# Row sums of exponentials in place of a clamp, values loaded one and a half times, constant matmuls ahead, and a new order by hand

## The chip, the cores and the metric

The kernel runs on one core of one Trainium2 chip. The metric is the time of one execution on the device in microseconds, the median of several runs. Smaller is better.

A core has engines that each work through a list of their own, in order: TensorE (PE in the profile) for matmuls and transposes, VectorE (DVE) and ScalarE (ACT) for elementwise work, GpSimd (POOL) for elementwise work too, and SyncE (SP), which here only issues DMA transfers and, at the end, reads a flag. An instruction waits for what it needs of other engines, and everything behind it on its own engine waits with it.

## The reference

Gated linear attention (a state per head, faded by a sigmoid gate at each step), and then a mixing block: angles, rotation by cosine and sine, mixing over tokens, and a channel product with a ReLU.

```python
f = 1.0 / (1.0 + np.exp(-f_logit))                  # B,H,S,D = 4,8,768,48
for t in range(S):
    state = f[:, :, t, :, None] * state + np.einsum('bhd,bhe->bhde', k[:, :, t], v[:, :, t])
    y[:, :, t] = np.einsum('bhd,bhde->bhe', q[:, :, t], state)
x = y.transpose(0, 2, 1, 3).reshape(B, S, H * D)    # 4, 768, 384
theta = x @ w_theta
zr, zi = x * np.cos(theta), x * np.sin(theta)
yr = np.einsum('ts,bsd->btd', w_tok_r, zr)
yi = np.einsum('ts,bsd->btd', w_tok_i, zi)
u = x + yr + yi
out = u + np.maximum(u @ w_ch, 0.0)
```

All inputs are float32 in value; the weights arrive as 64-bit floats and are decoded on the chip.

## The kernel before

The tokens of each of the four batches are cut into six chunks of 128, 24 in all, numbered through. The attention of a chunk m is written without a loop over time. The four head pairs lie side by side in tiles of 128 x 512.

- Gates: the logits f are loaded (`lf`), clamped from below (`gc`, `gate_clamp`, L236), turned into ln(1 + exp(-f)) by two activations (`go`, L241 and L242), summed along the chunk by a scan (`gs`, L246), and exponentiated twice (`ge`, L253 and L254) into p, the decay from the chunk's start, and its inverse, which overwrites f. `gp` (L257) keeps the last column of p in `pes`. q is multiplied by p (`gq`, L261), k by the capped inverse (`gk`, L266).
- Attention: transposes of k (`ke`, L308) and their copy (`kt`, through L143); scores (`sc`, L297) and their mask (`ma`, L303); sums of keys times values (`up`, L322); the state in the middle and at the end of the chunk (`sa`, L328 or L330, `st`, L334) and its fading (`sm`, L338); the outputs from the old state (`qs`, L353) and within the chunk (`ou`, L361); a copy (`xc`), transposes (`xt`, L371) and a copy into the tile `ut` of the group (`xs`). v of a chunk is one load of 384 KB (`lv`, L520) with two full copies of it in different head orders.
- Angles and rotation: the angle product (`th`, L402), rounding (`tn`, L407 on ScalarE or L409 on VectorE), remainder (`se`, L413), absolute value (`ab`, L418 on ScalarE or L420 on VectorE), two sines (`tr`), the product with x (`ro`, L435). From the second batch on the results are split into a high and a low float32r part (`zh`, `zl`).
- Mixing: `f0`, `f1`, `f2` (L458) are the token products of a chunk's rotated values for the three blocks of 128 columns, accumulated over the six chunks of a batch for one of two groups of 384 tokens. There are eight groups. The first batch multiplies in float32, the others as three float32r products. `v` (L462) adds, `uh` and `ul` (L469) split again, `c` (L476) is the channel product, `cv` (L490) the ReLU and sum, `so` (L494) one of three stores of a group.
- Weights: `lw`, `d1` (L182), `d2` (L187), `d3` (L192 and L193), `di` (L197), `d4`, `d5` (L217), `e4`, `e5` load and decode the weights piece by piece and split them.

What sets the order is a table written by hand, `ORDER`: a long row of these step names, each standing for the next chunk, group or piece of its kind; a suffix /P, /D or /A moves the step to GpSimd, VectorE or ScalarE. The program issues the steps in this order, and each engine keeps it.

The scaled products are exact only while the gates' range is moderate. `fl` (`find_worst`, L501 to L505) reduces `pes` on VectorE, compares, sums the comparison over partitions by a tiny matmul `pf`, and copies the result into `flag`. `rv` (L565) reads the flag into registers of the engines. If it is above zero a slow exact recurrence follows (the branch, L617), else nothing. Behind the branch the last group is stored by one DMA (L650):

```python
fn["rv"] = load_flag
for step in " ".join(ORDER).split():
    step, _, e = step.partition("/")
    m = done[step] = done.get(step, -1) + 1
    here[0] = engines[e]
    fn[step](m)
...
with tc.If(over[0] > 0, preferred_fallthrough_block=False):
...
nc.sync.dma_start(out[B - 1, :, S - TH:].rearrange("(k p) t -> p k t", p=P), uts[LAST])
```

In the trace an fp32 matmul shows as two records, a transpose and a float32r matmul as one; three or six lines of the table often merge into one row there.

## Time and profile before

| | |
|---|---|
| median of 3 runs | 340.54 us (339.99 to 340.63) |
| the profiled execution | 340.03 us |
| its span, first to last instruction | 338.3 us |
| TensorE busy | 320.4 us (95%) |
| VectorE busy | 251.6 us (74%) |
| ScalarE busy | 188.7 us (56%) |
| GpSimd busy | 108.6 us (32%) |
| DMA | 45.54 MB, mean 135 GB/s |

The shares are means over the whole span. The opening, the long stretch in which the products run, and the end have different limits, so the prediction reads stretches and timelines and not the means. A busy time is the time in which an engine's records cover the clock; matmuls overlap in the records, so the time of a block of them, not of one, tells their pace.

### The profile page before, as it was taken

How to read it: one execution, taken by the hardware profiler on the slowest of the kernel's cores; microseconds unless marked ns; L12 is line 12 of the kernel's file. 1: busy time of each engine (PE TensorE's matmuls, PEld its weight loads, DVE VectorE, ACT ScalarE, POOL GpSimd, SP SyncE). 2: the span in 40 equal slices, each digit the busy share in tenths (PEclk: the TensorE clock that was granted, in tenths of full speed). 3: DMA queues.
4: the chain of work that ended last, by engine and by line, in shares of the span. 5: the costliest groups of instructions: out<-in, count | busy, mean ns of one | idle time of the engine just before them, and what ended most of it. 6: DMA issues, size and time to landing. Idle time of an engine off the chain costs nothing. (4 is left out here: it accounts for less than half of the span.)

```text
span 338.3 us, 9998 instructions
## 1 busy us (share of the span) xinstructions
PE 320.4 (95%) x4320; PEld 283.2 (84%) x4320; DVE 251.6 (74%) x411; ACT 188.7 (56%) x308; POOL 108.6 (32%) x105
## 2 busy tenths in 40 slices
PE   0789999999999999999999999999999999999993
PEld 0676766776776789999999999999999999999992
DVE  5989999999999998898987857855437848534211
ACT  6787997995866755588476685244076114400010
POOL 3585152134418235701445423323212201300010
PEclk9999999999999999999999999999999999999998
DMA  7994994738761262374124320532121120000012
GB/s 256 382 401 168 317 372 151 249 114 323 244 224 30 64 230 82 91 233 141 33 85 149 122 79 2 187 114 84 40 73 48 47 73 27 0 2 0 11 60 78
DMA packets 21618, 45.54 MB, mean 135 GB/s; under 512 B 2368, under 2 KB 5440, under 8 KB 21568
## 3 DMA queue, kind: packets, MB, share of 16 engines
q1 hardware_dynamic: 21568, 44.84, 38.5%
q8 instruction: 36, 0.59, 0.7%
q14 instruction: 14, 0.11, 0.1%
HBM read 40.11 MB, written 4.72 MB: 133 GB/s over the span
## 5 line engine op out<-in xcount | busy, mean ns | idle before, releaser
L458 PE MATMUL pm<-wp,z 128*128 128x384 f32 x648 | 118.4, 337 | 0.0
L458 PEld LDWEIGHTS pm<-wp,z 128*128 128x128 f32 x648 | 112.4, 188 | 0.4
L458 PE MATMUL pm<-value,z 128*128 128x384 f32 x144 | 49.3, 487 | 0.0
L476 PE MATMUL pch<-uhl,wch 128*128 128x384 f32 x216 | 40.0, 337 | 0.0
L458 PEld LDWEIGHTS pm<-value,z 128*128 128x128 f32 x144 | 26.4, 190 | 15.2
L476 PEld LDWEIGHTS pch<-uhl,wch 128*128 128x128 f32 x216 | 37.4, 188 | 0.0
L469 POOL TENSOR_TENSOR uhl<-ut,uhl 128x384 fp32r<-128x384 f32 x13 | 14.2, 1094 | 67.0 <-ACT uhl L143 35.5
L236 POOL TENSOR_SCALAR f<-f 128x512 f32<-128x512 f32 x16 | 26.6, 1666 | 13.3 <-DMA f<-in_f_dram 12.5
L246 DVE TENSOR_TENSOR_SCAN f<-carry,f 128x512 f32<-128x512 f32 x24 | 29.8, 1246 | 1.4 <-ACT f L242 1.4
L257 POOL COPY pes<-p 128x4 f32<-128x4 f32 x24 | 10.5, 439 | 52.9 <-ACT p L253 52.9
L490 DVE SCALAR_TENSOR_TENSOR ut<-pch,ut 128x384 f32<-128x384 f32 x24 | 13.1, 550 | 18.8 <-PE pch L476 17.1
L308 PE MATMUL psk<-ident,k 128*128 128x128 f32 x96 | 16.9, 303 | 10.0 <-DVE k L266 10.0
L261 POOL TENSOR_TENSOR q<-q,p 128x512 f32<-128x512 f32 x12 | 17.3, 1446 | 23.1 <-ACT p L253 14.6
L462 DVE TENSOR_TENSOR ut<-pm,ut 128x384 f32<-128x384 f32 x24 | 13.0, 551 | 14.2 <-PE pm L458 14.2
L253 ACT ACTIVATE p<-f 128x512 f32<-128x512 f32 x24 | 15.1, 630 | 14.4 <-DVE f L246 6.8
L402 PE MATMUL pth<-wth,xh 128*128 128x384 f32 x108 | 23.0, 348 | 0.0
L308 PEld LDWEIGHTS psk<-ident,k 128*128 128x128 f32 x96 | 12.2, 153 | 12.3 <-issue 10.3
L435 DVE TENSOR_TENSOR w<-w,x 128x768 f32<-128x768 f32 x18 | 17.2, 962 | 6.3 <-ACT w L426 6.3
L143 ACT COPY x<-py 128x384 f32<-128x384 f32 x19 | 9.1, 478 | 22.5 <-PE py L361 22.1
L361 PEld LDWEIGHTS py<-v,sc 64*64 64x64 f32 x768 | 15.0, 140 | 7.4 <-issue 4.5
L143 ACT CAST uhl<-ut 128x384 fp32r<-128x384 f32 x7 | 3.6, 513 | 31.1 <-DVE ut L462 17.5
L266 DVE SCALAR_TENSOR_TENSOR k<-f,k 128x512 f32<-128x512 f32 x24 | 18.2, 758 | 1.8 <-ACT f L254 1.1
(83 smaller groups left out, 622.6 us busy)
## 6 DMA issues: line engine op xcount, KB each, us to landing
v<-in_v_dram SPq DMA_DIRECT2D x24, 384.0 KB, 4.3
f<-in_f_dram SPq DMA_DIRECT2D x24, 256.0 KB, 3.8
q<-in_q_dram SPq DMA_DIRECT2D x24, 256.0 KB, 4.1
k<-in_k_dram SPq DMA_DIRECT2D x24, 256.0 KB, 4.3
raw<-in_w_r_dram SPq DMA_DIRECT2D x12, 384.0 KB, 5.9
raw<-in_w_i_dram SPq DMA_DIRECT2D x12, 384.0 KB, 6.3
out_dram<-ut SPq DMA_DIRECT2D x21, 192.0 KB, 1.9
raw<-in_w_theta_dram SPq DMA_DIRECT2D x3, 384.0 KB, 6.4
```

The source lines that it names most:

```text
L236: on(nc.vector).tensor_scalar(ft, ft, F_MIN, None, op0=ALU.max)
L246: nc.vector.tensor_tensor_scan(fl, carry[:, pairs(h)].rearrange("p n t -> p (n t)"), fl, 0.0, ALU.mult, ALU.add)
L253: nc.scalar.activation(ps_[m][:, pairs(h)], ft, AF.Exp, scale=-1.0)
L261: on(nc.vector).tensor_tensor(qt, qt, ps_[m][:, pairs(h)], op=ALU.mult)
L266: nc.vector.scalar_tensor_tensor(kt, loaded["f", m][:, pairs(h)], E_TOP, kt, op0=ALU.min, op1=ALU.mult)
L308: nc.tensor.transpose(psks[m][:, p, :], loaded["k", m][:, p, :], ident)
L361: nc.tensor.matmul(out[HALF[t], j, p, :], scs[m][HALF[a], j, p, :], v2[HALF[a], t, p, :], start=(t == 0 and m % NC == 0 and p == 0), stop= ...
L402: nc.tensor.matmul(pths[m], l, r, start=(n == 0), stop=(n == len(ms) - 1))
L435: nc.vector.tensor_tensor(zs[m] if full else w, w, xs[m].unsqueeze(1).to_broadcast([P, 2, DM]), op=ALU.mult)
L458: nc.tensor.matmul(pms[g, d], l, r, start=(s == 0 and i == 0), stop=(s == NC - 1 and i == len(ms) - 1))
L469: on(nc.vector).tensor_tensor(us[g, d][:, 0], uts[g][:, d, :], us[g, d][:, 1], op=ALU.subtract)
L476: nc.tensor.matmul(pcs[g, d], l, r, start=(es[0] == 0 and n == 0), stop=(es[-1] == KD - 1 and n == len(ms) - 1))
```

## The change

- The clamp (`gc`) goes, 8 on VectorE and 16 on GpSimd. In its place the first exponential writes the sums of its rows (`accum_out`) into a new tile `opened`, and `find_worst` also takes the largest of these and compares it with `G_TOP`: on VectorE two small instructions more.
- p and the inverse change places: the inverse decay lies in p, the decay overwrites f.
- The first chunk's gates and its q and k are done in halves of two head pairs (steps with an h ahead).
- v of a chunk is loaded as three blocks of 192 columns in place of two of 384: 288 KB in place of 384.
- 30 matmuls of constants (`wu`, `keep_warm`, 128 x 128, float32) stand in the table ahead of the first angle product.
- The mask's result has two buffers in place of one; the decode step `d2` could run on VectorE, which the table doesn't use.
- `ORDER` is a new table. Among the steps with an engine: `ab/A` 12 to 13, `d4/D` 3 to 2, `d5/P` 5 to 6, `kt/D` 7 to 9, `sm/P` 11 to 13, `tn/D` 9 to 6, `uh/D` 17 to 13, `xs/D` 7 to 9, `zh/D` 8 to 10, `zl/P` 5 to 9, `di/D` 0 to 1. ScalarE loads its function tables 28 times in place of 22. `fl` stands just ahead of the last `c`, and of the 21 single stores two stand behind `rv`, at the very end.

```diff
-F_MIN = -44.0
+G_TOP = 1e18
-CUT = 0
+CUT = 1
 ORDER = (
-    "lf gc lf gc go go gs lf gc/P lq lk lv gs ge gq gp go ge gk lw lk gs ke kt up gp sc lq gq/P d1 lw lq d2 gk ke",
...
-    "f2 f2 ul so f2 cv cv c cv uh ul/P f2 v uh c c ul/P so c so so so rv cv cv cv",
+    "hlf hgo wu wu wu wu lf go hlf hgo hgs hge wu wu wu wu wu wu wu wu gs hlk hlq hlk hgs hgk hge hgk lf ke wu wu",
...
+    "v uh/D ul cv f1 f2 f2 f2 f1 f1 f1 f1 f1 f2 f2 so v c cv c f2 cv c uh/D ul/P v uh/D ul c gp fl c rv cv cv cv",
+    "so so",
 )
+    opened = const.tile([P, B * NC + 1], F32, tag="opened", name="opened")
-    def gate_clamp(m, h=None):
-        ft = loaded["f", m][:, pairs(h)]
-        on(nc.vector).tensor_scalar(ft, ft, F_MIN, None, op0=ALU.max)
-
     def gate_open(m, h=None):
-        nc.scalar.activation(ft, ft, AF.Exp, scale=-1.0)
+        n = B * NC if h else m
+        nc.scalar.activation(ft, ft, AF.Exp, scale=-1.0, accum_out=opened[:, n:n + 1])
         nc.scalar.activation(ft, ft, AF.Ln, bias=1.0)
-        nc.scalar.activation(ps_[m][:, pairs(h)], ft, AF.Exp, scale=-1.0)
-        nc.scalar.activation(ft, ft, AF.Exp)
+        nc.scalar.activation(ps_[m][:, pairs(h)], ft, AF.Exp)
+        nc.scalar.activation(ft, ft, AF.Exp, scale=-1.0)
-        scs[m] = sb.tile([P, 2, NP, HF], F32, tag="sc", bufs=1, name=f"sc{m}")
+        scs[m] = sb.tile([P, 2, NP, HF], F32, tag="sc", bufs=2, name=f"sc{m}")
+    def keep_warm(n):
+
+        nc.tensor.matmul(bank([P, C], f"warm{n}"), ident, carry[:, 1], start=True, stop=True)
+
-    worst = const.tile([P, 2], F32, tag="worst", name="worst")
+    worst = const.tile([P, 3], F32, tag="worst", name="worst")
     def find_worst(_):
         nc.vector.tensor_reduce(worst[:, 0:1], pes, axis=AX.XY, op=ALU.min)
-        nc.vector.tensor_scalar(worst[:, 1:2], worst[:, 0:1], E_MIN, None, op0=ALU.is_lt)
+        nc.vector.tensor_reduce(worst[:, 1:2], opened, axis=AX.X, op=ALU.max)
+        nc.vector.tensor_scalar(worst[:, 0:1], worst[:, 0:1], E_MIN, None, op0=ALU.is_lt)
+        nc.vector.scalar_tensor_tensor(worst[:, 2:3], worst[:, 1:2], G_TOP, worst[:, 0:1], op0=ALU.is_gt, op1=ALU.add)
         pf = bank([P, 1], "pf")
-        nc.tensor.matmul(pf[:1, :], ones, worst[:, 1:2], start=True, stop=True)
+        nc.tensor.matmul(pf[:1, :], ones, worst[:, 2:3], start=True, stop=True)
         nc.vector.tensor_copy(flag[:1, :], pf[:1, :])
-        vs[m] = sb.tile([P, 2, DM], F32, tag="v", bufs=3, name=f"v{m}")
+        vs[m] = sb.tile([P, 3, NP * D], F32, tag="v", bufs=3, name=f"v{m}")
```

Three places of the order follow, a row for each instruction or run of like ones.

VectorE at the start, before: behind four constants come two clamps and two scans, then q and k of the first chunk; `mid` is the copy of the first sums.

```order
L236 TENSOR_SCALAR f_92<-f_92 128x512
L236 TENSOR_SCALAR f_95<-f_95 128x512
L246 SCALAR_TENSOR_TENSOR f_92<-carry,f_92 128x512
L246 SCALAR_TENSOR_TENSOR f_95<-carry,f_95 128x512
L261 TENSOR_TENSOR q_107<-q_107,p_114 128x512
L266 SCALAR_TENSOR_TENSOR k_109<-f_92,k_109 128x512
L246 SCALAR_TENSOR_TENSOR f_104<-carry,f_104 128x512
L182 TENSOR_SCALAR raw_125<-raw_125 128x768
L266 SCALAR_TENSOR_TENSOR k_128<-f_95,k_128 128x512
L328 COPY mid_191<-sk 128x192
```

VectorE at the start, now, up to the same copy (L329); `ktok` is the copy of the transposed k, `raw` and `value` are pieces of weights.

```order
L248 SCALAR_TENSOR_TENSOR f_93<-carry,f_93 128x256
L248 SCALAR_TENSOR_TENSOR f_106<-carry,f_106 128x512
L248 SCALAR_TENSOR_TENSOR f_93<-carry,f_93 128x256
L268 SCALAR_TENSOR_TENSOR k_134<-p_114,k_134 128x256 x2
L268 SCALAR_TENSOR_TENSOR k_158<-p_177,k_158 128x512
L263 TENSOR_TENSOR q_136<-q_136,f_93 128x256
L145 COPY ktok_195<-psk_146 128x512
L184 TENSOR_SCALAR raw_166<-raw_166 128x768
L248 SCALAR_TENSOR_TENSOR f_144<-carry,f_144 128x512
L197 SCALAR_TENSOR_TENSOR raw_166<-raw_166 128x768
L198 SCALAR_TENSOR_TENSOR value_214<-raw_166 128x768
L329 COPY mid_256<-sk 128x192
```

The clamps are gone and the first scan works on half; between the scaled k of chunk 1 and the copy of the first sums there now stand a copy, a decode, a scan and a join pair.

TensorE at the start, before: transposes of k of chunk 0, its sums and scores, transposes of chunk 1, and so on.

```order
L308 MATMUL psk_131<-ident,k_109 128x128 x4
L322 MATMUL sk<-v_111,ktok_136 64x48 x16
L297 MATMUL sk_156<-q_107,k_109 64x64 x16
L308 MATMUL psk_184<-ident,k_128 128x128 x4
L353 MATMUL py_216<-mid_191,q_107 64x48 x8
L322 MATMUL sk_156<-v_205,ktok_200 64x48 x16
```

TensorE at the start, now, from the last of twelve constant matmuls on; `warm` is their result, which nothing reads; of the nine between the two transposes the first and the last are shown.

```order
L501 MATMUL warm_131<-carry,ident 128x128
L310 MATMUL psk_146<-ident,k_134 128x128 x4
L501 MATMUL warm_151<-carry,ident 128x128
...
L501 MATMUL warm_175<-carry,ident 128x128
L310 MATMUL psk_188<-ident,k_158 128x128 x4
L323 MATMUL sk<-v_171,ktok_195 64x48 x16
L299 MATMUL sk_229<-q_136,k_134 64x64 x16
L501 MATMUL warm_246<-carry,ident 128x128
L354 MATMUL py_263<-mid_256,q_136 64x48 x8
L323 MATMUL sk_229<-v_180,ktok_254 64x48 x16
```

The transposes of chunk 1 moved ahead of the sums of chunk 0, and the constant matmuls stand between.

SyncE near the end, before: the last single stores, then the flag and the branch.

```order
L494 DMA out_dram<-ut_2157 128x384 x3
L494 DMA out_dram<-ut_2856 128x384 x3
L494 DMA out_dram<-ut_3272 128x384 x3
L565 TENSOR_LOAD flag
L565 ISA x2
L617 COMPARE_AND_BRANCH
```

SyncE near the end, now.

```order
L496 DMA out_dram<-ut_2167 128x384 x3
L496 DMA out_dram<-ut_2843 128x384 x3
L496 DMA out_dram<-ut_3310 128x384
L573 TENSOR_LOAD flag
L573 ISA x2
L496 DMA out_dram<-ut_3310 128x384 x2
L625 COMPARE_AND_BRANCH
```

Two stores of the group before the last moved behind the flag, and stand between it and the branch. On TensorE the little matmul of the flag, which stood among the token products of the last group, now stands nine matmuls ahead of the last one:

```order
L478 MATMUL pch_4375<-uhl_4383,wch_88 128x384
L478 MATMUL pch_4379<-uhl_4383,wch_88 128x384
L478 MATMUL pch_4379<-uhl_4383,wch_87 128x384
L478 MATMUL pch_4379<-uhl_4383,wch_88 128x384
L512 MATMUL pf<-worst,ones 1x1
L478 MATMUL pch_4371<-uhl_4387,wch_88 128x384
```

Behind it are only the channel products of the last split part.

## Rows read from the trace of the kernel before

**Rows 1.** Stretches: busy us (x instructions) of PE, PEld, DVE, ACT, POOL; clock; DMA; GB/s.

```profile
9.50:31.20 21.70, 19.21 (x329) 14.46 (x329) 19.92 (x30) 16.78 (x29) 13.64 (x12) 1.00 0.90 343
31.20:60.00 28.80, 28.72 (x567) 19.78 (x570) 27.55 (x46) 24.43 (x39) 9.91 (x11) 1.00 0.74 253
60.00:120.00 60.00, 59.86 (x761) 42.67 (x753) 59.22 (x87) 45.23 (x74) 22.94 (x21) 1.00 0.54 184
120.00:200.00 80.00, 80.00 (x1250) 76.82 (x1249) 67.57 (x112) 53.60 (x88) 32.62 (x28) 1.00 0.38 125
```

**Rows 2.** Timeline of the end, all engines: start us, us, engine, line, operation.

```profile
327.59 0.33 SPq L494 DMA_DIRECT2D out_dram<-ut  x1
...
327.79 4.84 PE L476 MATMUL pch<-uhl,wch 128*128 128x384 f32 x27
...
333.43 0.39 SPq L650 DMA_DIRECT2D out_dram<-ut  x1
```

**Rows 3.** Timeline of PE around 31 us: the first two angle products' blocks.

```profile
27.09 4.19 PE L402 MATMUL pth<-value,ut 128*128 128x384 f32 x6
...
34.54 2.20 PE L402 MATMUL pth<-value,ut 128*128 128x384 f32 x6
```

**Rows 4.** Waits of PE up to 31.2: us in total, times, longest.

```profile
PE psk L308 <- DVE k L266: 10.0, 2, 9.6
```

**Rows 5.** Stretches again (columns as in group 1), up to 71.34.

```profile
0.00:71.34 71.34, 59.26 (x1038) 41.87 (x1042) 63.87 (x102) 58.06 (x95) 29.18 (x36) 1.00 0.77 274
```

**Rows 6.** Costliest groups by form: count | busy us, mean ns | idle before.

```profile
L246 DVE TENSOR_TENSOR_SCAN f<-carry,f 128x512 f32<-128x512 f32 x24 | 29.8, 1246 | 1.4 <-ACT f L242 1.4
L236 POOL TENSOR_SCALAR f<-f 128x512 f32<-128x512 f32 x16 | 26.6, 1666 | 13.3 <-DMA f<-in_f_dram 12.5 <-DVE k L266 0.8
...
L266 DVE SCALAR_TENSOR_TENSOR k<-f,k 128x512 f32<-128x512 f32 x24 | 18.2, 758 | 1.8 <-ACT f L254 1.1 <-DMA k<-in_k_dram 0.6
...
L226 ACT ACT_TABLE_LOAD x11 | 14.1, 1283 | 1.0 <-PEq L689 0.8
...
L192 DVE SCALAR_TENSOR_TENSOR raw<-raw 128x768 int32<-128x768 int32 x14 | 13.7, 980 | 0.0
...
L261 DVE TENSOR_TENSOR q<-q,p 128x512 f32<-128x512 f32 x12 | 8.6, 715 | 0.8 <-ACT p L253 0.8
...
L420 DVE TENSOR_SCALAR w<-w 128x384 int32<-128x384 int32 x12 | 5.6, 465 | 0.2
L409 DVE TENSOR_SCALAR w<-pth 128x384 f32<-128x384 f32 x9 | 4.9, 548 | 0.4 <-PE pth L402 0.4
...
L236 DVE TENSOR_SCALAR f<-f 128x512 f32<-128x512 f32 x8 | 3.5, 442 | 4.9 <-DMA f<-in_f_dram 4.9
L338 DVE TENSOR_TENSOR st<-st,pes 128x192 f32<-128x192 f32 x9 | 3.2, 357 | 0.0
```

**Rows 7.** Timeline of DVE, two operations beside GpSimd.

```profile
5.52 2.71 DVE L246 TENSOR_TENSOR_SCAN f<-carry,f 128x512 f32<-128x512 f32 x2 [0.75 <-ACT f L242]
...
30.25 1.69 DVE L266 SCALAR_TENSOR_TENSOR k<-f,k 128x512 f32<-128x512 f32 x1
```

**Rows 8.** Timeline of POOL up to 72 us: clamps and a scaling of q.

```profile
6.41 1.61 POOL L236 TENSOR_SCALAR f<-f 128x512 f32<-128x512 f32 x1 [4.51 <-DMA f<-in_f_dram]
...
29.65 1.74 POOL L261 TENSOR_TENSOR q<-q,p 128x512 f32<-128x512 f32 x1 [0.67 <-DMA q<-in_q_dram]
...
67.06 1.48 POOL L236 TENSOR_SCALAR f<-f 128x512 f32<-128x512 f32 x1
```

**Rows 9.** SyncE's steps at L565, L617, L650; last, landing of L494's stores.

```profile
L565 SPq TENSOR_LOAD <-flag x1: 492/492/492, 328.0 to 328.0; - x1
...
L617 SPq EVENT_SEMAPHORE  x8: 17/17/17, 328.9 to 329.8; - x8
...
L650 SPq EVENT_SEMAPHORE  x5: 17/28/2772, 330.4 to 330.6; - x5
...
DMA to landing us min/median/max: 1.8/1.9/5.2
```

More of the change, by code (lines that the diff above doesn't have):

```diff
@@ L356, in att_out @@
     def att_out(m):
-        out, v2 = y_of(m), vs[m][:, 1, :].rearrange("s (t p e) -> s t p e", t=2, p=NP)
+        out = y_of(m)
         for n, (p, t) in enumerate(OUT):
@@ L360, in att_out @@
                 j = a ^ t
-                nc.tensor.matmul(out[HALF[t], j, p, :], scs[m][HALF[a], j, p, :], v2[HALF[a], t, p, :],
+                nc.tensor.matmul(out[HALF[t], j, p, :], scs[m][HALF[a], j, p, :],
+                                 vs[m][HALF[a], 2 * j, p * D:(p + 1) * D],
                                  start=(t == 0 and m % NC == 0 and p == 0), stop=(p == NP - 1))
@@ L559, in gla_moe_kernel @@
         "f0": piece(0), "f1": piece(1), "f2": piece(2), "v": group(add_u), "uh": group(split_uh), "ul": group(split_ul), "c": channels, "cv": group(finish),
-        "so": group(lambda g, d: store(g // NTH, g, d)), "fl": find_worst,
+        "so": group(lambda g, d: store(g // NTH, g, d)), "fl": find_worst, "wu": keep_warm,
     }
@@ L664, in layout @@
     halves = v.transpose(0, 2, 1, 3).reshape(B, NC, 2, HF, NP, 2, D)
-    rolled = np.stack([np.stack([halves[:, :, t, :, :, a ^ t] for t in range(2)], axis=3) for a in range(2)], axis=2)
-    v2 = np.stack([halves.reshape(B, NC, C, DM), rolled.reshape(B, NC, C, DM)], axis=3)
-    v2 = np.ascontiguousarray(v2)
+    parts = [halves[..., 0, :], halves[..., 1, :], halves[:, :, ::-1, :, :, 1, :]]
+    v2 = np.ascontiguousarray(np.stack([a.reshape(B, NC, C, NP * D) for a in parts], axis=3))
     return {
```

16 lines of the change are left out of this document (9 added, 7 removed), and 66 rows, old and new, of the table ORDER.

## Prediction

> **What bounds the kernel now.** I read the table of stretches first. From 31.2 us on, TensorE is busy 28.72 of 28.80, 59.86 of 60 and 80.00 of 80 us [rows 1], and so to its last matmul, in the block that starts at 327.79 and runs 4.84 us [rows 2]. Time can therefore be won in three ways only: TensorE starts its full stretch earlier, it has less to do, or the end behind its last matmul gets shorter. The change takes no matmul away and adds 30, so the two ends decide.
>
> The second view is TensorE's timeline around 31 us. The angle product of one chunk (L402, three fp32 matmuls 128x384, each of which makes two records) takes 4.19 us at 27.09 and 2.20 us at 34.54 [rows 3]. The granted clock column reads 1.00 in both stretches [rows 1], so it doesn't show the step; the durations do. I read them as the lower of TensorE's two levels (1.2 GHz) up to 31.2 us and the upper (2.4 GHz) after it. TensorE's waits before that are small: two for scaled k, 10.0 us in sum, of which 9.6 stand before its first matmul [rows 4].
>
> The third view is VectorE in the same stretches: 19.92 of 21.70, 27.55 of 28.80, 59.22 of 60, and only after 120 us 67.57 of 80 [rows 1]. So for a third of the run VectorE is as full as TensorE. An earlier TensorE meets the same VectorE, and what it wins stays only as far as VectorE has less to do for the same matmuls. This is the step on which the forecast rests.
>
> **VectorE's list up to one point.** At 71.34 us of before TensorE starts the scores of chunk 7, and VectorE, with 102 instructions (four of them constants) begun, was busy 63.87 us of it [rows 5]. In the new order TensorE has as much work behind it (45.7 us of matmul time at the upper level, by counting both orders, the 30 constant ones left out) when it comes to the outputs of chunk 6, for which VectorE must have done 94 instructions. By kinds, at the mean of one [rows 6]: four clamps at 0.442 less (1.77); one scan at 1.246 less (ten, now eight and two halves); one scaling of k at 0.758 less; three roundings L409 at 0.548 less (1.64), and a copy of the same shape; one fade L338 at 0.357 less; one weight split, at the 0.980 of a join. Together 7.3 us less. More are 1.5 scalings of q at 0.715 (1.07), two joins of a decoded weight at 0.980 (1.96), one L420 and one scaling of a weight, both at 0.465 (0.93). Together 4.0 more. That leaves 3.3 us; but the last instruction that before had begun by then (a q, 0.7) was not needed yet, so I count 2.6. The same count at other points up to 120 us gives 2 to 6, so this is near the least, and the least binds.
>
> **The clamps on GpSimd** go too, 16 at 1.666, 26.6 us [rows 6]. GpSimd itself is not awaited on the path, so they give nothing directly. But VectorE is slower beside it: two scans at 5.52 take 2.71, where two means make 2.49, beside the clamp at 6.41; a scaling of k at 30.25 takes 1.69 instead of 0.758 beside a scaling of q at 29.65, a kind that stays [rows 7, 8]. Up to 71 us eight clamps run there, the last at 67.06 [rows 8]. The relief lies between 0 (the next GpSimd operation slides into the gap) and some 1.5 (0.2 for each as the scans show). I take 0.6, a little under the middle, since GpSimd has other work to put there.
>
> The Trainium skill ("SBUF — State Buffer", Who interferes with whom) states a harder rule: VectorE and GpSimd share one pair of ports, and for an instruction that needs it the other engine is fully blocked while it is held. By it eight clamps would have held VectorE for up to 13 us, and this sum would be rival B at its fullest; the scans beside the clamp lost 0.2 and not 1.6, so the trace doesn't agree as far as that operation goes.
>
> **Other parts of the opening.** The first chunk's gates in halves take out a clamp (0.44), half a scan (0.62) and half a k (0.38) before the first matmul [rows 6], so it comes about 1.5 us earlier, at some 8 us. I don't add this: VectorE's first work still waits for the first f, and the list above already holds it. The 30 constant matmuls are fp32, 128x128: a record three times as wide takes 4.19/6 = 0.70 at the lower level [rows 3], so by my estimate one of them is 2 x 0.23 = 0.47 there and 0.24 at the upper, all of them 14 or 7 us. All stand ahead of the first angle product, where TensorE would mostly wait: twelve before the first transposes of k, from some 1.7 us (the constants are there) to 7.3 at the lower level, nine between the first and the second. If the twelve bring the clock up, the nine take 2.1 and end by the time the second k is scaled, and are free; if not, 4.2, which delays the first sums (rival D). With the clock up, VectorE's own waits for TensorE shrink as well: of its 1.8 us of idle time between 9.5 and 31.2 [rows 1] I take a quarter, 0.4, between nothing and all. v's loads shrink by a quarter; DMA, 0.90 busy there [rows 1], gets room, worth nothing where no load is awaited. ACT gets six more table loads at 1.283 [rows 6], 7.7 us at most on 58.06 of 71.34 [rows 5]: 65.8, still under 68, so hidden. The row sums that the exponential now writes have no row; their price is between 0 and the 0.465 of a small VectorE instruction each, on ACT, hidden likewise; I take 0. Opening: 2.6 + 0.6 + 0.4 = **3.6 us won**.
>
> **The end.** In before the flag has long been computed when SyncE gets to it: it sends the last store of the group before the last (327.59), loads the flag at 328.0, stands in its branch at 328.9, has the stores' landings by 330, waits on L650's semaphores from 330.4 [rows 9], and sends the last store at 333.43, 5.64 after the last 27 matmuls began [rows 2]. All of it lies under TensorE and VectorE. In the new order the worst-case check stands 18 matmuls into these 27, with nine behind it: 18/27 of 4.84 is 3.2 after their begin. The flag's copy and hand-over add 0.25. Then SyncE loads it and gets through in 0.9 (328.0 to 328.9 [rows 9]): 4.4. Only now come two stores, 0.33 to 0.4 each to issue, the second at 4.8; it lands 1.9 later [rows 9], at 6.7. The branch's way out waits for all DMA queues, so it is this landing. From the landing of before (327.59 + 1.9 = 329.5) to the L650 semaphores it took 0.9 to 1.1; so the last store goes out at 7.7, against 5.64. VectorE's last finishing step, which set the 5.64 in before, no longer counts. Cost: **2.1 us**, between 1.7 (landing 0.2 sooner, hand-overs free) and 2.6 (the flag's load on VectorE also delays the finishing steps). Two instructions more in the check cost nothing: they fall under the 18 matmuls.
>
> **Sum.** 340.03, the profiled run, less 3.6, plus 2.1: 338.5. The profiled run lies 0.5 under the median 340.54; carried over to that, **339.0 us**.
>
> **Rivals.**
> A, the forecast: opening 2 to 5, so 337.6 to 340.6.
> B, VectorE doesn't bind: its 1.8 us of idle time close altogether, and the relief is all of 1.5. 2.6 + 1.8 + 1.5 = 5.9 won, 2.1 lost: 336.7. For it speaks that constant matmuls bring the clock up early; against it that VectorE's list is nearly all in series there. The rule of the ports in the skill, named above, would lead here.
> C, slower: VectorE holds TensorE at the old pace, because of one place. Before the copy of the first sums (mid, L328, now L329), the new order puts a decode, a scan and a join pair: 0.65 + 1.25 + 1.96 = 3.9 us [rows 6] (the decode at about two thirds of a join), and the first reads of the state wait behind it. What the list saves is spent by that, the late flag costs its 2.1 and nothing covers it: 342.1 at 0.5 won, 342.6 at none. It decides from the point where the opening gives less than 2.1.
> D, the constant matmuls don't do what they are there for: TensorE stays at its lower level through the first angle product, which then takes 4.2 again [rows 3], and the nine constants take 4.2, so that the 1.5 us of the earlier start are gone before the first sums. Of the opening a third is left, 1.2; 2.1 is lost: 341.4. For it speaks that 15 us of transposes and narrow products before 27.09 (19.21 busy of 21.70, the angle product's 4.1 off [rows 1]) did not raise the clock; against it that the twelve would run without a gap, as the wide products do when the clock rises at 31.2. The skill ("TensorE: Matmul & The Clock Gate", What's actually happening) says that the throttled state is the default and activity releases it; by this the row of before should have been fast earlier than it is, and the trace agrees only in part.
>
> **Chances.** A 0.50, B 0.16, C 0.21, D 0.13. About 0.2% is what a measurement of this kernel can tell from no change: 0.7 us, so faster is below 339.9, slower above 341.2. From A 0.37 fall faster, 0.11 same, 0.02 slower; B is all faster; C 0.17 slower and 0.04 same; D 0.05 same, 0.08 slower. Faster 0.53, same 0.20, slower 0.27. The range runs from 336.4 (B, with the end at 1.8) to 342.3 (C); left out are more than B and the full C with an end of 2.6, 0.15 or so. The likeliest case's own range is 337.6 to 340.6.
>
> **What would show it.** In the trace of after: the first angle product shorter than 2.3 us and starting by about 24 (else D); VectorE's busy share up to 70 us still above 0.9, with TensorE waiting for mask, mid or scaled k (else B); VectorE's scans and k beside GpSimd nearer their means; TensorE's last matmul about 3.6 us earlier; from that to the last store's issue 2.9 instead of 0.8 us, with SyncE in its branch waiting for a store that it issued after the flag. It is wrong if TensorE's waits after 31 us exceed 1 us in sum, or if the last store goes out right after VectorE's last step.

## The result, and the profile after

The changed kernel takes 342.32 us (median of 20 runs, 341.05 to 344.91), the kernel before 340.10 in 20 runs beside it: 1.0072 times as long, 95% interval 1.005 to 1.0095. It is slower by 2.2 us, where 339.0 and a gain were forecast. Two things are to be explained: the end, where two stores now stand behind the flag, and the opening, whose forecast gain of 3.6 us is not in the time. The profiled execution took 343.98 with a span of 341.6, so it is one of the longer ones.

Busy times of the whole span come first (share, instructions). They say little, as in the kernel before: TensorE 95% again, VectorE 4 us less, ScalarE 11 us more, GpSimd 15 less.

```profile
PE 324.7 (95%) x4380; PEld 288.7 (85%) x4380; DVE 247.5 (72%) x398; ACT 199.3 (58%) x345; POOL 94.0 (28%) x97
```

The end is where the clearest loss lies. In the timeline of all engines from 326 us on (start, duration, engine, line; line numbers are those of the changed kernel) the check's little matmul stands between the 18th and the 19th of the last 27 channel products, the two single stores go out at 331.55, and the last store only at 335.77:

```profile
327.06 3.28 PE L478 MATMUL pch<-uhl,wch 128*128 128x384 f32 x18
...
330.27 0.19 PE L512 MATMUL pf<-worst,ones 128*1 128x1 f32 x2
...
330.39 1.83 PE L478 MATMUL pch<-uhl,wch 128*128 128x384 f32 x9
330.50 0.15 DVE L513 CAST flag<-pf 1x1 int32<-1x1 f32 x1 [0.94 <-PE pf L512]
331.31 1.50 DVE L492 SCALAR_TENSOR_TENSOR ut<-pch,ut 128x384 f32<-128x384 f32 x3 [0.67 <-PE pch L478]
331.55 0.81 SPq L496 DMA_DIRECT2D out_dram<-ut  x2
335.77 0.39 SPq L658 DMA_DIRECT2D out_dram<-ut  x1
```

TensorE ends at 330.39 + 1.83 = 332.22, so 0.41 earlier than before (332.63 by [rows 2]); but the last store goes out 3.55 us behind that, against 0.80 there. The row of SyncE's waits says that it stood in the branch (L625, L617 before) in between. The row doesn't name a transfer, but the second of the two stores, out at 332.0, landed at 334.8, and the branch's last semaphore went at 334.9. That this landing is what it waited for is tested by e3 below.

```profile
SPq L625 <- SPq L625: 2.0, 2, 1.2
```

From the last store's issue to the end of the span it takes 5.8 us, against 4.9 before. Together the end is 3.7 us longer.

The opening has to be read in short stretches (columns as in [rows 1]: busy time of PE, PEld, DVE, ACT, POOL; granted clock; DMA share; GB/s):

```profile
8.00:12.00 4.00, 3.20 (x25) 2.72 (x24) 1.75 (x4) 2.60 (x6) 0.88 (x2) 1.00 1.01 354
12.00:15.00 3.00, 1.60 (x67) 1.32 (x66) 2.34 (x3) 1.54 (x2) 0.00 (x0) 1.00 1.07 403
15.00:17.00 2.00, 0.00 (x0) 0.03 (x1) 1.83 (x5) 1.89 (x5) 1.56 (x1) 0.80 0.98 344
17.00:19.00 2.00, 1.99 (x49) 1.91 (x49) 1.16 (x3) 1.32 (x4) 2.00 (x3) 0.50 0.83 289
19.00:21.00 2.00, 2.00 (x12) 1.67 (x16) 2.00 (x5) 0.01 (x1) 0.41 (x2) 0.50 0.88 257
21.00:23.00 2.00, 2.00 (x65) 1.91 (x66) 1.97 (x5) 1.10 (x3) 0.00 (x0) 0.50 0.34 124
23.00:26.00 3.00, 3.00 (x79) 2.70 (x79) 1.40 (x4) 2.97 (x6) 0.19 (x1) 0.99 0.04 15
26.00:32.00 6.00, 6.00 (x145) 4.61 (x145) 5.97 (x9) 5.50 (x13) 1.16 (x2) 1.00 1.01 345
```

The clock column now has something to show. Up to 15 us it is 1.00 and the matmuls have the upper pace (32 narrow ones in 0.68 us below, 1.10 in the kernel before). From 15 to 17 TensorE does nothing. Then the clock is 0.50, the lower of the two levels, until 23 us, while TensorE is busy all the time. The timeline of TensorE shows the pause and whom it waited for, that of VectorE why:

```profile
13.37 0.68 PE L323 MATMUL sk<-v,ktok 64*64 64x48 f32 x32 [1.35 <-DMA v<-in_v_dram]
13.87 0.66 PE L299 MATMUL sk<-q,k 48*64 48x64 f32 x32
...
17.01 0.77 PE L354 MATMUL py<-mid,q 48*64 48x48 f32 x10 [2.06 <-DVE st L335]
...
27.61 2.10 PE L404 MATMUL pth<-value,ut 128*128 128x384 f32 x6
```

```profile
12.66 0.57 DVE L184 TENSOR_SCALAR raw<-raw 128x768 int32<-128x768 int32 x1 [2.07 <-DMA raw<-in_w_theta_dram]
13.14 1.22 DVE L248 TENSOR_TENSOR_SCAN f<-carry,f 128x512 f32<-128x512 f32 x1
14.27 0.93 DVE L197 SCALAR_TENSOR_TENSOR raw<-raw 128x768 int32<-128x768 int32 x1
15.24 0.96 DVE L198 SCALAR_TENSOR_TENSOR value<-raw 128x768 int32<-128x768 int32 x1
16.12 0.35 DVE L329 COPY mid<-sk 128x192 f32<-128x192 f32 x1
```

VectorE's copy of the first sums (L329) could have gone at 14.05, when the products of L323 were there. It went at 16.12, because a decode (L184) ahead of it waited 2.07 us for the load of a weight, and a scan and two joins stand between. These are the four instructions that rival C named. TensorE's first sums had themselves waited 1.35 us, for the load of v. The first angle product runs at the upper level (2.10 us, 4.19 in [rows 3]), but at 27.61, where 24 was expected; it ends 1.6 us earlier than before.

How far TensorE is ahead at any time can be counted. Each matmul record of a trace gets the time that it takes in a closed row at the upper level (0.3225 us for an fp32 record 384 wide, 0.1735 for a float32r one, 0.109 for a transpose, some 0.015 for a narrow one, nothing for a constant one). This gives 299.3 us of work in every kernel here. The work done at a time, less that of the kernel before at the same time, is the lead, in us:

| at | after | e2 | e6 | e3 | e4 | e7 | e11 | e12 |
|---|---|---|---|---|---|---|---|---|
| 26 | -0.9 | 0.8 | 1.1 | -0.4 | -0.3 | 1.8 | 1.8 | -1.2 |
| 44 | 1.7 | 3.7 | 3.4 | 2.4 | 0.8 | 4.3 | 3.7 | -0.4 |
| 62 | 1.7 | 2.7 | 2.0 | 2.1 | 0.4 | 3.5 | 3.5 | -0.1 |
| 112 | 0.9 | 2.4 | 1.6 | 0.9 | -0.2 | 3.5 | 3.5 | -0.8 |
| 136 | 0.7 | 2.1 | 0.2 | 0.7 | -0.4 | 1.2 | 2.4 | -0.8 |
| 328 | 0.7 | 1.2 | 0.0 | 0.5 | -1.2 | 1.0 | 2.4 | -1.0 |

Each column is one execution. The changed kernel, e2 and e3 have the same order up to the last products, and still e2 is up to 2.0 us ahead of the other two. Its TensorE makes the same pause (2.0 us), but its granted clock is 0.86 from 19 to 21 us and 1.00 from 21 on, where the changed kernel has 0.50 until 23. So how long the lower level lasts differs between executions of one order, and a difference of less than 2 us between columns says something only where a wait in the traces stands behind it.

### The profile page after: what moved, and what is told of

It is laid out like the page before. It is cut to its first block, busy times and chain, and to the rows that moved or that the text cites. A ratio compares the mean times of both kernels' runs of the same rounds, so it can differ in the third digit from the quotient of the medians.

```text
span 341.6 us, 10162 instructions
## 1 busy us (share of the span) xinstructions
PE 324.7 (95%) x4380; PEld 288.7 (85%) x4380; DVE 247.5 (72%) x398; ACT 199.3 (58%) x345; POOL 94.0 (28%) x97
## 4 chain that ended last, share of the span: by engine, by line
PE 85%; DVE 5%; DMA 4%; SPq 2%; issue 1%; DVEq 0%
PE pm L460 45%; PE pch L478 11%; PE pth L404 10%; PE py L362 4%; PE py L354 3%; PE sk L299 3%; PE psk L310 3%; PE sk L323 3%; PE pxt L373 2%; DMA raw<-in_w_theta_dram 2%; DMA raw<-in_w_i_dram 2%; SPq L523 1%; SPq L171 1%; PE warm L501 1%; DVE value L198 1%
## 5 line engine op out<-in xcount | busy, mean ns | idle before, releaser
L471 POOL TENSOR_TENSOR uhl<-ut,uhl 128x384 fp32r<-128x384 f32 x13 | 16.3, 1257 | 75.2 <-DVE uhl L145 61.0
L248 DVE TENSOR_TENSOR_SCAN f<-carry,f 128x512 f32<-128x512 f32 (+1 forms) x25 | 31.1, 1253 | 3.7 <-ACT f L244 3.7
L263 POOL TENSOR_TENSOR q<-q,f 128x512 f32<-128x512 f32 (+1 forms) x13 | 19.7, 1518 | 41.2 <-DMA q<-in_q_dram 17.4
L437 DVE TENSOR_TENSOR w<-w,x 128x768 f32<-128x768 f32 x18 | 20.4, 1140 | 4.7 <-ACT w L428 4.5
L259 POOL COPY pes<-f 128x4 f32<-128x4 f32 x24 | 7.8, 326 | 53.9 <-ACT f L256 43.8
L444 POOL TENSOR_TENSOR z<-w,z 128x768 fp32r<-128x768 f32 x9 | 17.3, 1926 | 18.3 <-ACT z L145 14.0
L255 ACT ACTIVATE p<-f 128x512 f32<-128x512 f32 (+1 forms) x25 | 15.3, 612 | 9.2 <-DVE f L248 9.0
L268 DVE SCALAR_TENSOR_TENSOR k<-p,k 128x512 f32<-128x512 f32 (+1 forms) x25 | 17.5, 700 | 3.0 <-ACT p L255 2.0
L404 PEld LDWEIGHTS pth<-wth,xh 128*128 128x128 f32 x108 | 18.7, 188 | 0.9
L354 PE MATMUL py<-mid,q 48*64 48x48 f32 x384 | 16.6, 227 | 2.1 <-DVE st L335 2.1
```

The source lines that it names most:

```text
L248: nc.vector.tensor_tensor_scan(fl, carry[:, pairs(h)].rearrange("p n t -> p (n t)"), fl, 0.0, ALU.mult, ALU.add)
L263: on(nc.vector).tensor_tensor(qt, qt, loaded["f", m][:, pairs(h)], op=ALU.mult)
L268: nc.vector.scalar_tensor_tensor(kt, ps_[m][:, pairs(h)], E_TOP, kt, op0=ALU.min, op1=ALU.mult)
L354: nc.tensor.matmul(out[HALF[t], j, p, :], qt[r, p, HALF[t]], old[t][r, p, :], start=(p == 0), stop=False)
L404: nc.tensor.matmul(pths[m], l, r, start=(n == 0), stop=(n == len(ms) - 1))
L437: nc.vector.tensor_tensor(zs[m] if full else w, w, xs[m].unsqueeze(1).to_broadcast([P, 2, DM]), op=ALU.mult)
```

## The end: e3, e2

Only the two stores moved, the check stays late:

```diff
-    "... uh/D ul/P v uh/D ul c gp fl c rv cv cv cv",
-    "so so",
+    "... uh/D ul/P v uh/D ul so so c gp fl c rv cv cv cv",
```

> The changed kernel with the two last single stores moved ahead of the reading of the flag, the check staying late (nine matmuls ahead of the end). Theory 2a (the two stores behind the flag are the price: the branch waits for their landing): nearly all of what the earlier end gives, 2.3 us or more less than the changed kernel, last store about 1 us behind the last matmul. Rival (the late flag is the price by itself): at most 0.8 less, last store over 2 us behind the last matmul.

339.35 us (337.75 to 340.44, 12 runs), 2.97 under the changed kernel and 0.998 of the kernel before (0.9958 to 1.0002). Its timeline of the end (its lines are one less than in the changed kernel):

```profile
325.29 1.90 SPq L495 DMA_DIRECT2D out_dram<-ut  x2
...
330.35 0.19 PE L511 MATMUL pf<-worst,ones 128*1 128x1 f32 x2
...
330.47 1.83 PE L477 MATMUL pch<-uhl,wch 128*128 128x384 f32 x9
...
331.39 1.50 DVE L491 SCALAR_TENSOR_TENSOR ut<-pch,ut 128x384 f32<-128x384 f32 x3 [0.67 <-PE pch L477]
333.04 0.39 SPq L657 DMA_DIRECT2D out_dram<-ut  x1
```

The flag is as late as in the changed kernel, and the last store goes out 0.74 us behind the last matmul. It is the two stores behind the flag that cost, not the flag. With the check moved early too:

```diff
-    "c f2 ro zh/D f1 zl f1 f2 f2 f0 f0 v v f2 cv v so ...
+    "c f2 ro zh/D f1 zl f1 f2 f2 f0 f0 v v f2 gp fl cv v so ...
-    "... uh/D ul/P v uh/D ul c gp fl c rv cv cv cv",
-    "so so",
+    "... uh/D ul/P v uh/D ul so so c c rv cv cv cv",
```

> The changed kernel with the end of the kernel before: the check of the range (and the copy of the last chunk's decay that it needs) stands among the last token products, and all 21 single stores stand ahead of the reading of the flag. Theory 2 (the end of the changed kernel costs 3.7 us: from TensorE's last matmul to the last instruction 9.4 in place of 5.7): 3 to 3.7 us less than the changed kernel, last store 0.8 us behind the last matmul. Rival (the final transfer is slower for another reason, its landing took 4.9 in place of 3.7): 2.1 to 2.7 less, and the landing stays near 4.9.

339.47 (337.36 to 341.40, 12 runs), 0.9997 of the kernel before (0.9974 to 1.0021): the same as e3. So the two stores behind the flag are the loss at the end, and the flag itself is not (theory 2a). By these medians the end costs the changed kernel 2.9 to 3.0 us; set against the kernel before that ran beside each (340.10 beside the changed kernel, 339.64 beside these two) it is 2.4 to 2.5. The transfer at the very end, 5.8 us from issue to the end of the span, is 5.1 in both, so most of its lengthening goes with the stores as well; why is not shown.

## TensorE's level: e4, b1, e6

All 30 constant matmuls taken out of e3 (every `wu` in the table):

> The changed kernel with its two last single stores ahead of the flag (as in e3_so_only, 339.35) and without any of the 30 constant matmuls. Theory 1 (the constant matmuls lift TensorE's level at about 8 us and win some 3 us ahead of the first angle product, part of which is kept): the first angle product runs at the lower level (about 4.1 us), the time is 1 to 3 us above e3_so_only. Rival (VectorE and the loads set the pace of the opening, TensorE's level is worth nothing): within 0.7 of e3_so_only.

342.19 (10 runs), 2.8 above e3, or 2.4 with each set against the kernel before beside it (340.04 here, 339.64 there). The first angle product of its trace:

```profile
27.82 2.81 PE L403 MATMUL pth<-value,ut 128*128 128x384 f32 x6
```

It takes 2.81 us where the changed kernel has 2.10 and the kernel before 4.19: by this the level rises in the middle of it. The constant matmuls are worth 2.4 to 2.8 us here: in the lead, 1.6 us at 44 and 1.7 at the end. The mirror of it, twelve of them put at the start of the kernel before:

```diff
-    "lf gc lf gc go go gs ...
+    "lf gc wu wu wu wu wu wu wu wu wu wu wu wu lf gc go go gs ...
```

> The kernel before with twelve constant matmuls ahead of its first transposes and nothing else. Theory 1: TensorE's level is up by about 8 us, the first angle product at 27 takes 2.1 in place of 4.2 us or comes earlier, and 1 to 2 us are won against the kernel before. Rival 1 (the level falls again in the first pause, since the rest of the opening has pauses once it runs fast): the granted clock falls back to 0.50 before 20 us, gain under 0.7. Rival 2 (VectorE sets the pace): level stays up, gain under 0.7.

340.26 against 340.04 (ratio 0.9989 to 1.0032): nothing. The stretches of its trace show why:

```profile
8.00:12.00 4.00, 1.78 (x30) 1.41 (x32) 3.64 (x6) 3.79 (x7) 0.86 (x3) 0.64 1.03 403
12.00:15.00 3.00, 3.00 (x66) 2.55 (x64) 2.46 (x6) 1.60 (x4) 1.72 (x2) 0.50 1.05 400
...
26.00:32.00 6.00, 5.76 (x48) 3.26 (x49) 6.00 (x8) 4.28 (x9) 3.13 (x3) 0.50 0.44 164
```

TensorE paused 3.0 us for the first scaled k, the clock fell within 8 to 12 us and stayed at 0.50 past 26. So early matmuls alone don't keep the level up: here, too, it fell behind a pause. That the pause and not their number (12 here, 30 there) decides is argued, not shown.

Eight more constant matmuls in the changed kernel, in TensorE's pause:

```diff
-    "d3 ge kt sa st lv sm qs gp gk ...
+    "d3 ge kt sa st lv sm wu wu wu wu wu wu wu wu qs gp gk ...
```

> The changed kernel with eight constant matmuls more, where TensorE waits for the first state (in front of the first outputs from the state). The wait of VectorE stays as it is. Theory 1: TensorE is busy through 15 to 17 us, the granted clock stays 1.00, the products from 17.0 to 23.8 take half of their time, and the first angle product comes 1 to 3 us earlier; time 1 to 3 us less than the changed kernel. Rival 1 (VectorE alone sets the pace): clock 1.00, but no gain over 0.7 us at the end. Rival 2 (the level falls for another reason than the pause): the granted clock still drops to 0.50 at about 17.

The first half came true:

```profile
15.00:17.00 2.00, 1.40 (x12) 1.41 (x12) 1.86 (x5) 1.92 (x5) 2.00 (x3) 1.00 1.05 418
17.00:19.00 2.00, 2.00 (x57) 1.83 (x57) 1.23 (x3) 0.71 (x2) 1.80 (x2) 1.00 0.92 307
19.00:21.00 2.00, 1.67 (x69) 1.40 (x67) 2.00 (x5) 1.14 (x3) 0.00 (x0) 1.00 0.69 255
```

The clock stays at 1.00, and the first angle product comes at 25.49, 2.1 us earlier than in the trace of the changed kernel. (In e2's trace, whose lower level was short, it comes at 25.68 without the eight matmuls.) But the time is 344.20, 1.9 us more than the changed kernel. No theory had that. VectorE's waits from 24 to 130 us say where the first 1.4 go (waited for, times, longest):

```profile
DVE q L263 <- DMA q<-in_q_dram: 1.9, 2, 1.4
```

The scaling of q of chunk 5 waits for its load at 46 us, where DMA is 1.00 busy from 40 to 44. Set against the changed kernel instruction by instruction, VectorE is 2.1 us ahead at 25 to 36, 1.5 at 37 and 0.6 from 46 on. At 119 us it falls behind, after a wait of 1.84 us on ScalarE for a load of f. In this execution being early only meant waiting there. It explains that nothing is won; the trace ends 0.6 us behind that of the changed kernel, and why the medians differ by 1.9 stays open.

In the 20 runs of the changed kernel the time goes with the level all the same: the mean granted clock over the span tells how long it was low. The six runs at 0.982 to 0.984 take 344.1 in the mean, the eight at 0.988 to 0.990 take 341.5. What else differs between these runs isn't known.

## The first state moved ahead: e1, e10, e12

If the pause is VectorE's wait for the weight, the copy of the sums could go first:

```diff
-    "... hgq ke lk kt/D up d1 lq lq gq/P gs lf lw lw sc wu d2",
-    "d3 ge kt sa st lv sm qs ...
+    "... hgq ke lk kt/D up lq lq gq/P lf lw lw sc wu sa st d1 gs d2",
+    "d3 ge kt lv sm qs ...
```

> The changed kernel with one edit: on VectorE the copy of the first sums and the first state (sa, st) stand ahead of the weight decode, scan and joins (d1, gs, d3), as in the kernel before. Theory 1 (the opening was lost to one wait: TensorE stood from 15.0 to 17.0 us because VectorE's copy of the first sums stood behind a decode that waited 2.1 us for a weight load, and then ran at its lower level to 23.8): the copy comes at about 14.1 in place of 16.1, the granted clock stays 1.00 from 8 to 31 us, and the time falls by 1.5 to 4 us against the changed kernel, to 338.5 to 341 where that has 342.3. Rival (VectorE's list sets the pace in any case, so TensorE's clock there is worth nothing): the first angle product comes earlier, but at the end less than 0.7 us is left.

345.77 (5 runs): 3.4 slower than the changed kernel, both theories wrong. The longest wait of TensorE is now another:

```profile
PE sk L323 <- ACT ktok L145: 3.7, 1, 3.7
```

The scan (`gs`) had moved behind the state, ScalarE's exponentials wait for the scan, and the copy of k's transposes stands behind them. So I put the scan back, and the exponentials and the copy ahead on ScalarE, with the stores of e3:

```diff
-    "... hgq ke lk kt/D up d1 lq lq gq/P gs lf lw lw sc wu d2",
-    "d3 ge kt sa st lv sm qs ...
+    "... hgq ke lk kt/D up lq lq gq/P gs lf lw lw sc wu ge kt sa st d1 d2",
+    "d3 lv sm qs ...
```

> As e3_so_only (339.35), with the copy of the first sums and the first state ahead of the decode and the joins on VectorE, and on ScalarE the exponentials and the copy of k's transposes ahead of the decode's scaling, so that neither stands behind a wait for the weight load (in e1_mid_first the scan and, by it, the copy of k's transposes had been put behind the state, and TensorE waited 3.7 us for that). Theory 1: VectorE's copy of the first sums at about 14.2 in place of 16, no pause of TensorE over 1 us between 12 and 24, the granted clock 1.00 there, and at 62 us 1 us or more further ahead than e3_so_only; time 0.5 to 1.5 us less. Rival (the next products wait for the scaled k or for v instead): a pause of over 1 us elsewhere before 24 and no gain.

341.69, 2.3 slower than e3. The same kernel ran once more, for a trace:

> The same as e10_mid_scan (341.7), for its trace, since the profile of that run was of a disturbed execution. Theory 1 fell there by the time. Theory 5 (what counts is the order in which VectorE gets at the next scaled k and scan, not the first state: with the decode and joins later, the weights are later and the first angle product waits for them): no pause of TensorE between 14 and 17 us, but the first angle product at or after 27.6 with a wait for a weight or for its inputs. Rival (the clock): the granted clock falls to 0.50 before 24 us although the pause at 15 to 17 is gone.

341.99. The copy of the first sums comes at 13.72, 2.4 us earlier than in the changed kernel. What comes then, on VectorE and on GpSimd:

```profile
13.72 0.36 DVE L328 COPY mid<-sk 128x192 f32<-128x192 f32 x1 [1.48 <-PE sk L322]
14.12 0.36 DVE L334 TENSOR_TENSOR st<-sk,mid 128x192 f32<-128x192 f32 x1
...
15.19 1.98 DVE L196 SCALAR_TENSOR_TENSOR raw<-raw 128x768 int32<-128x768 int32 x1 [0.24 <-ACT raw L189]
17.20 2.05 DVE L197 SCALAR_TENSOR_TENSOR value<-raw 128x768 int32<-128x768 int32 x1
...
19.44 0.68 DVE L267 SCALAR_TENSOR_TENSOR k<-p,k 128x512 f32<-128x512 f32 x1
```

```profile
15.08 1.27 POOL L262 TENSOR_TENSOR q<-q,f 128x512 f32<-128x512 f32 x1 [5.84 <-DMA q<-in_q_dram]
16.29 0.92 POOL L258 COPY pes<-f 128x4 f32<-128x4 f32 x1
17.17 1.26 POOL L262 TENSOR_TENSOR q<-q,f 128x512 f32<-128x512 f32 x1
18.38 0.91 POOL L258 COPY pes<-f 128x4 f32<-128x4 f32 x1
```

The two joins take 1.98 and 2.05 us in place of 0.93 and 0.96, each beside a scaling of q on GpSimd. So the scaled k that TensorE needs next goes at 19.44, where the changed kernel had it at 17.47. TensorE waits 3.8 us for it (16.4 to 20.2), and the clock falls to 0.50 from 19 to 24. The first angle product comes at 28.79. The pause only moved, so the level wasn't spared here. In the changed kernel the order is the other way round: the first join is through when q begins on GpSimd at 15.44, the second, issued at 15.24, keeps 0.96, and the q beside it takes 1.89 in place of 1.27. The first theory's cause (the level falls behind a pause) fits these runs as well; its remedy was wrong.

## Where the lead goes: e7, e8, e11

e7 is e3 with the eight matmuls of e6 and the load of q of chunk 5 ahead of two pairs of weight loads:

```diff
-    "... lf sm/P sc sa st lw sm/P qs se ab/A d3 tr ro up sa xt go ma go th lw",
-    "f1 tn d3 f0 gs lq xs lw gq ge ...
+    "... lf sm/P sc sa st lq lw sm/P qs se ab/A d3 tr ro up sa xt go ma go th lw",
+    "f1 tn d3 f0 gs xs lw gq ge ...
```

> As e3_so_only, with the eight constant matmuls of e6_more_wu, and with the load of q of chunk 5 moved ahead of two pairs of weight loads on SyncE's queue. In e6_more_wu TensorE's level stayed up and the first angle product came 2.1 us earlier, but VectorE gave 0.6 back at about 35 us and 0.9 at 46, waiting for loads of q. Theory 3 (what the opening wins is given back to loads that come too late, DMA being 1.00 busy from 40 to 44 us): the wait of 1.4 us at 46 is gone, and VectorE is still 1.5 us ahead of e3_so_only at 60 us; time 1 to 2 us under e3_so_only, 337.4 to 338.4. Rival (another load takes its place, DMA as a whole is the limit): a weight load comes late in its turn, and the time is within 0.7 of e3_so_only.

339.93, 0.6 above e3 (0.2 with each set against the kernel before beside it) and 1.001 of the kernel before (0.9985 to 1.0036). By the time, the rival is the one that held; the trace says more. The wait at 46 us is gone, and the lead is 4.3 us at 44 and 3.5 up to 112, the 3.6 that the forecast gave the opening. By 136 it is 1.2. The timeline between, all engines:

```profile
112.97 2.74 POOL L443 TENSOR_TENSOR z<-w,z 128x768 fp32r<-128x768 f32 x1
...
115.66 0.92 POOL L258 COPY pes<-f 128x4 f32<-128x4 f32 x1
...
116.60 0.33 SPq L522 DMA_DIRECT2D f<-in_f_dram  x1
117.02 0.86 SPq L495 DMA_DIRECT2D out_dram<-ut  x2
...
118.04 0.78 PE L403 MATMUL pth<-wth,xl 128*128 128x384 f32 x3 [0.92 <-POOL xl L394]
...
119.87 0.63 ACT L242 ACTIVATE f<-f 128x512 f32<-128x512 f32 x1 [3.08 <-DMA f<-in_f_dram]
...
120.96 0.56 DVE L144 COPY ut<-pxt 128x384 f32<-128x384 f32 x1 [0.89 <-DMA out_dram<-ut]
```

On GpSimd the small copy of a decay (L258) stands behind a split of 2.74 us. A load of f waits for that copy, to get a free buffer, and goes out at 116.60. Behind it on SyncE stand two stores whose data was ready by 114.6. So ScalarE waits 3.08 us for f and VectorE 0.89 for the stores; TensorE waits 0.92 for another split, which stands behind the same copy on GpSimd. Two ways to mend it. First the copy ahead of the split and the stores ahead of the load:

```diff
-    "... v e5 e5 sm zl/P gp v qs xt go gs go c xs",
+    "... v e5 e5 sm gp zl/P v qs xt go gs go c xs",
-    "... uh/D tn/D se lf so so xt go f2 ge",
+    "... uh/D tn/D se so so lf xt go f2 ge",
```

> As e7_q_early, with two steps of the table moved: two single stores of the first group ahead of a load of f that waits on SyncE for GpSimd's copy of a decay (pes), and that copy ahead of a long split on GpSimd. In e7_q_early TensorE had done 3.5 us more work than in the kernel before at 112 us, and 1.5 at 124: VectorE waited 0.9 us for the stores' landing, ScalarE 3.1 us for the load, TensorE 0.9 for a split behind both. Theory 3 (the opening's gain of 3.6 to 4 us was there, and is given back at single waits for transfers): the lead at 124 is 3 us or more, and the time falls by 1 to 2 us against e7_q_early (339.9), to 338 to 339. Rival (TensorE's lead runs into VectorE's list anyway, as the prediction had it): another wait takes its place by 130 us, less than 0.7 us.

339.83, the same. ScalarE still waited 2.60 us: the load now stood behind the stores, which wait for the ReLU. Then the copy alone (the first of the two edits):

> As e7_q_early with one step moved: the copy of a decay (pes) ahead of a long split on GpSimd, so that the load of f that waits for it on SyncE can go out before the two single stores of the first group and not behind or beside them (in e8_stores_first the stores went ahead and ScalarE still waited 2.6 us for that load). Theory 3 (the opening's lead is given back at single late transfers, here the f at 120 us): ScalarE's wait for f at about 118 is under 1 us, the lead over the kernel before at 136 us is 2.5 us or more (1.2 in e7_q_early), and the time 1 to 2 us under e7_q_early (339.9), so 338 to 339. Rival (VectorE and GpSimd, both full there, take what the load gives): lead at 136 under 1.7, time within 0.7.

338.81 (12 runs; 337.73 to 342.50). ScalarE's row that answers to the one at 119.87:

```profile
117.58 0.63 ACT L242 ACTIVATE f<-f 128x512 f32<-128x512 f32 x1 [0.65 <-DMA f<-in_f_dram]
```

The wait is 0.65, and the lead of 2.4 us at 136 is still there at 328. For that place the lead bears theory 3 out: from 112 to 136 us e7 falls from 3.5 to 1.2 and this run from 3.5 to 2.4. Two other traces point the same way. In e6 the split takes 2.74 us as well, the load goes out at 117.87, and the lead falls from 1.6 to 0.2; in e2 the split takes 1.85, the load goes out at 115.15, and 2.1 of 2.4 are kept. In the time this gain is not shown: the median is 1.1 under that of e7, but the kernel before beside it is lower too (339.59, and 340.04 beside e7), and the intervals of the two ratios overlap. Against the kernel before this best version has a median 0.8 lower, but three of its runs are above 340.5, and the ratio is 0.9998 (0.9964 to 1.0031); that it is faster is not shown.

## Parts alone: b2, b3, e9

The kernel before without its 24 clamp steps:

> The kernel before without its clamp steps (24 gate clamps, 8 on VectorE and 16 on GpSimd, left out; nothing checks the range in their place). This is the part of the change that the prediction priced at 1.77 us of VectorE's list up to 71 us and 0.6 us of relief from GpSimd. Theory (VectorE's list sets the pace of the first 120 us): 1 to 2.4 us less than the kernel before. Rival (loads set it, or TensorE's lower level): within 0.7 of it.

339.90 against 340.04 (0.9967 to 1.0017): nothing like the 2.4 us that the forecast gave. Its profiled execution (342.88) is the slowest of the twelve, so it shows only one way in which a shorter list can be lost: TensorE waits 2.5 us for a scaled k, until 33.0. VectorE is busy throughout from 27 to 33, and one addition to the state, issued at 29.79 beside a scaling of q on GpSimd (1.28 us), takes 1.45 us in place of 0.36. The granted clock is 0.50 from 34 to 38. By the medians, fewer instructions on VectorE did not make this kernel shorter.

The kernel before with v in three blocks (the change's `load_v`, its two readers and the layout):

> The kernel before with one part of the change alone: v of a chunk loaded as three blocks of 192 columns (288 in place of 384 KB), its order untouched. Prediction: v's smaller loads are worth nothing where no load is awaited: within 0.7 of the kernel before, and outside of the span 1.7 us as in the kernel before. Rival 1 (the DMA engines limit the opening of the kernel before as well): 1 us or more less. Rival 2 (the 0.6 us outside of the span come with v's new shape): 2.3 to 2.4 us outside of the span.

339.76 against 339.59 (0.9983 to 1.004): nothing, as forecast; 1.8 us outside of the span, so the shape of v isn't what lengthens that part. Its first angle product takes 3.11 us and that of b2 2.20, where [rows 3] has 4.19: with the old order, too, the level comes up earlier in one execution than in another.

e3 without the row sums:

```diff
-        nc.scalar.activation(ft, ft, AF.Exp, scale=-1.0, accum_out=opened[:, n:n + 1])
+        nc.scalar.activation(ft, ft, AF.Exp, scale=-1.0)
```

> As e3_so_only, without the row sums that the first exponential writes (left out; the check then looks at a constant in their place). In the changed kernel each of these exponentials is followed by a record of 0.19 us on ScalarE, and the device time is 2.4 us above the span in place of 1.7. Theory 4 (the row sums are free, hidden on ScalarE): within 0.7 of e3_so_only (339.35), and the 0.6 us outside of the span stay, so they belong to something else. Rival: ScalarE's 25 records count on the path, or the part outside of the span comes with them: 0.6 us or more less.

338.50 and 0.9973 of the kernel before (0.9948 to 0.9999), where e3 has 339.35 and 0.998 (0.9958 to 1.0002). The medians lie 0.85 apart, the ratios some 0.2 us, and the intervals overlap. In the changed kernel the row sums have a record of their own on ScalarE:

```profile
L243 ACT ACTIVATION_READ_ACCUMULATOR f<-f 128x1 f32 x25 | 4.7, 188 | 0.0
```

That they cost anything isn't shown: the lead in the profile of this kernel (0.3 at 328, e3 0.5) doesn't show it either. The part outside of the span stayed at 2.4.

## Why the prediction was wrong

**The end.** The mechanism was right: the flag's chain ran as told (pf at 330.27, 3.21 into the 27 products; the stores at 331.55, 4.5), and the branch waited for the second store. The size was off: 3.55 us from matmul to last store, not 2.9, because the second store, out at 332.0, took 2.8 us to land and not 1.9, and the branch's last semaphore went at 334.9; and the last transfer took 0.9 longer, which the forecast did not have. Priced at 2.1, with 2.6 as its highest, the end is 3.7 longer in the traces and 2.4 to 3.0 by the medians of e2 and e3.

**The opening.** Priced at 3.6, it is 0.7 at the end of the trace, and by medians, e3 against before, 0.3, or 0.9 with the 0.6 us outside of the span put aside. The step that failed is the one on which the forecast rested: counting VectorE's list up to one point and taking the saving as time. VectorE's list did get shorter, but the time went idle instead. The stretches up to 70 us, before and after, show it:

```profile
0.00:70.00 70.00, 57.92 (x979) 40.69 (x980) 62.56 (x100) 56.80 (x92) 29.18 (x36) 1.00 0.78 279
0.00:70.00 70.00, 62.49 (x1042) 46.47 (x1042) 59.14 (x99) 56.41 (x105) 12.36 (x27) 0.95 0.78 262
```

VectorE is busy 3.4 us less, and its share, which was to stay above 0.9, is 0.84 (0.89 before). It waited instead: 2.07 us for a weight, with TensorE behind it. The pause that this made on TensorE is followed by the lower level for some 6 us, a term that the sum did not have. The clamp's removal, priced at 1.77 and 0.6, changes nothing that can be told in the kernel before (b2). That waits at the head of the queues and the lower level held the gain back is supported by e7, which takes out the pause and one wait and is 3.5 us ahead up to 112 us; that the gain can be had as time, no run shows.

**The loads.** "Worth nothing where no load is awaited" was the wrong way round for the new order: a weight at 12.7, v at 13.4, in e6 a q at 46 and in e7 an f at 118 were awaited. For q and f, moving them, or what they waited for, in the order took all or most of the wait away (e7, e11); for the weight and v this was not tried. I had looked at the amount of the traffic and not at the places of the loads.

**Rivals C and D.** D was half right: the level did come up (32 narrow matmuls in 0.68 us at 13.37), and fell again behind a pause that I had listed under C without its effect on the clock. C's place, the decode ahead of the first sums, is where the pause came from, and its 342.1 to 342.6 holds the time that was measured. In part that is luck: C counted the length of four instructions where a wait for a load and the lower level did it, and the end cost more than its 2.1. That the 30 matmuls are worth much was right: 2.4 to 2.8 us.

**The ports.** I set aside the rule of the Trainium skill ("SBUF — State Buffer", Who interferes with whom) for the scans beside the clamp. The runs agree with it more than I allowed: a join takes 1.98 in place of 0.98 beside a q on GpSimd, a scan 2.28 in place of 1.25 in e1, and where the join went first it was the q that took longer (after). In these cases the one issued first kept its time, or nearly, and the other paid.

**Six tenths outside.** The device time exceeds the span by 2.3 to 2.4 us in the mean of every kernel with the new order and by 1.7 to 1.8 in every one with the old. It isn't the constant matmuls (e4), the row sums (e9), the stores (e3) or v (b3). What it is stays open.

The time itself lay just above the range, which ended at 342.3.

## What to carry to other kernels

On queues in order, look for what waits at the head of each queue in the new order, loads first, before counting what became shorter. A gain at the start of a run can be lost again at one later load that doesn't go out earlier too; follow it with a count of work done at fixed times, against the old trace, and with more than one trace of each kernel. Put no transfer between a flag and a branch that the last transfer has to get through.
